# The first batch's columns by 16-bit halves and a transposing DMA, and three rows of the second batch's mixing by summands

## The chip, the cores and the metric

The kernel runs on one core of a Trainium2 chip (trn2). The engines that matter here are TensorE (PE: matmuls and transposes, its weight loads shown as PEld), VectorE (DVE), ScalarE (ACT), GpSimd (POOL) and SyncE (SP, which issues DMAs). Each engine works through its own instructions in the order of the program and waits for others by semaphores, each wait being a count that another engine's semaphore has to reach. The metric is the device time of one execution in microseconds (us).

## The reference

Three layers run one after the other on two batches of 768 tokens with 512 channels. Cut to what matters:

```python
# attention: q, k, v (2, 8, 768, 64); a key is kept if global (pos < 8) or local (0 <= rel < 96)
x = attention(q, k, v).transpose(0, 2, 1, 3).reshape(B, S, 512)

def _moe_ref(x, w_tok1, w_tok2, w_ch1, w_ch2):     # the second layer
    xt = x.transpose(0, 2, 1)
    h = np.maximum(xt @ w_tok1, 0.0) @ w_tok2      # mixes the 768 tokens, through 256
    u = x + h.transpose(0, 2, 1)
    h2 = np.maximum(u @ w_ch1, 0.0) @ w_ch2        # mixes the 512 channels, through 1536
    return u + h2

def _moe2_ref(x, w_theta, w_tok_r, w_tok_i, w_ch): # the third layer
    theta = x @ w_theta
    y = w_tok_r @ (x * cos(theta)) + w_tok_i @ (x * sin(theta))
    u = x + y
    return u + np.maximum(u @ w_ch, 0.0)
```

The change lies in the second layer, between `u` (after the token mixing) and `u @ w_ch1`. That product contracts over channels, so TensorE needs `u` with channels on the partitions, that is, the columns of `u`, while `u` itself has tokens on the partitions.

## The kernel before, in words

A float32 number is kept as two halves, a high one and a low one (the rest), and a product is three matmuls, high by high, high by low and low by high (`mm3`, L96). The rows of each batch stay in SBUF as `x[b]`, six blocks s of 128 tokens by 512 channels.

**Attention and token mixing.** The program tests the two counts in the inputs and takes the band branch or the dense branch of an If; these inputs take the band branch. Its work is a list of N units, and the work of the second layer that is ready is put between them as fills. For batch b, `token_part` makes `mm1` (`mm1_b_tb`, two halves tb of 256, contraction over the six blocks); at its end ScalarE makes the high half of `h1[b]` (L706) and VectorE the low one (L708). `token_row` then makes one block of rows `mm2_b_s`, six matmuls over two summands t, and VectorE adds it into `x[b]` (L768). For batch 0 all of this lies inside the branch. For batch 1, `mm1` is the end of the branch and `mm2` stands behind the If, in `token_mix2`.

**Columns.** For batch 0, `turn_row` lets TensorE transpose a block of rows, four transposes of 128 by 128 into one PSUM tile `ut_0_s` (L799), and ScalarE and VectorE split it into the high and low half of the columns, `ut[0]` (`evac_split`, L706 and L712; the memory is that of `xh0` and `xl0`, and the rows carry these names). Blocks 0 to 3 are fills, blocks 4 and 5 stand behind the last matmul of `mm1`. For batch 1 the columns come later, in `channel_mix`, in another way: `columns_out` lets POOL cut the 32-bit words into two planes of 16-bit halves (L779) and SP issue a transposing DMA (L783), `halves_join` lets POOL put the halves together again (L789), and `columns_split` makes the high half by a ScalarE cast (L792) and the low one by a VectorE subtraction (L793).

**Channel mixing.** `channel_mix` makes, for each of twelve steps k, `gp_b_k_0` (512 columns of `ut[b]`, blocks 0 to 3, 12 matmuls) and `gp_b_k_1` (256 columns, blocks 4 and 5), each evacuated by ScalarE and VectorE into `g` (L706, L708). Both use the PSUM tag `t`, which has two buffers; attention's transposes (L484) and `ut` use the same tag. Then come 18 matmuls of the second product, `h2`.

**What sets the order.** The program is written under a manual schedule: each engine takes its instructions as the code emits them. The weights are converted to halves by jobs: `job_scale` (ScalarE, L139 and L140), `job_join` (VectorE L145 and L148, then POOL L149), `job_high` (ScalarE L157), `job_low` (VectorE L160). Each `tick` emits the next phase of the running jobs and begins another. Behind the If, `token_mix2` ticks after rows 1, 3 and 5, and `channel_mix` after each evacuation. Behind the If the semaphore counts are the same whichever branch was taken.

The functions that the change touches, and what calls them:

Of the kernel before, what the change touches and what calls it, by code (L numbers as in the profile page):

```python
# [83 lines left out]
class Build:  # L84
# [326 lines left out]
    def attention_band(self, pairs_pool, first, h1):  # L411
# [6 lines left out]
        with tc.tile_pool(name="au", bufs=2) as up, tc.tile_pool(name="aa", bufs=2) as ap:  # L418
# [127 lines left out]
            def columns(s):  # L546
                return functools.partial(self.turn_row, "t", 0, s)

# [5 lines left out]
            for s in range(4):  # L554
                fill[N - 2 + s].append(columns(s))
# [47 lines left out]
            for s in range(4, NS):  # L603
                columns(s)()

    def attention_dense(self, pairs_pool, first, h1):
# [4 lines left out]
        with tc.tile_pool(name="du", bufs=2) as up, tc.tile_pool(name="dm", bufs=1) as mp:  # L611
# [86 lines left out]
            for s in range(NS):  # L698
                self.token_row("m", h1, 0, s)
                self.turn_row("t", 0, s)  # L700
# [52 lines left out]
    def token_row(self, tag, h1, b, s):  # L753

        ps = self.ps.tile([P, E], F32, name="mm2_%d_%d" % (b, s), tag=tag)
        cs = slice(s * P, (s + 1) * P)
        self.mm3(
# [12 lines left out]
    def turn_row(self, tag, b, s):  # L770
        h, s0 = divmod(s * P, E)
        hi, lo = (t[h][:, :, s0 : s0 + P] for t in self.ut[b])
        self.turn_rows(tag, self.x[b][:, s, :], r(hi), r(lo), "ut_%d_%d" % (b, s))
# [20 lines left out]

    def turn_rows(self, tag, src, hi, lo, name):

        pt = self.ps.tile([P, NE, P], F32, name=name, tag=tag)
        for d in range(NE):
            self.nc.tensor.transpose(pt[:, d, :], src[:, d * P : (d + 1) * P], self.ident)  # L799
        self.evac_split(hi, lo, pt)  # L800
# [66 lines left out]
    def run(self):  # L867
        nc, tc, dram = self.nc, self.tc, self.dram
        with ExitStack() as es:
# [13 lines left out]
            self.mm1 = {}  # L883
# [109 lines left out]
    def moe(self, es, a8s, w12p, h1):  # L993
        tc = self.tc
        ws = es.enter_context(tc.tile_pool(name="ws", bufs=1, side="right"))
        self.moe_jobs(ws, w12p)
        self.prefetch()
# [7 lines left out]
    def token_mix2(self, h1):  # L1005
        for s in range(NS):
            self.token_row("acc", h1, 1, s)
            if s % 2:
                self.tick()

    def columns_out(self, pb, s):
        t = self.turning[s] = pb.scratch("ut_%d" % s, ("cut", "xt0", "xt1")[s % 3])
        self.halves_out(self.x[1][:, s, :], t, self.nc.gpsimd.tensor_copy)

    def columns_split(self, s):
        h, s0 = divmod(s * P, E)
        hi, lo = (u[h][:, :, s0 : s0 + P] for u in self.ut[1])
        self.halves_split(self.turning.pop(s), r(hi), r(lo))
# [343 lines left out]
```

## Time and profile before

| | before |
|---|---|
| median of 3 runs | 497.35 us (497.07 to 498.65) |
| the profiled execution | 497.5 us, of which the span is 495.7 us |
| TensorE busy | 486.2 us, 98% of the span |
| VectorE, ScalarE, POOL busy | 312.6, 264.8, 180.8 us |
| mean granted TensorE clock | 0.996 |
| attention ends, second layer goes on behind the If | about 115 us |

The profile is one execution of the kernel. Its page sums the engines, follows the chain that ended last back through what released each piece, and groups the instructions by line. From the same trace come views of a stretch: the timeline (one row for one or more equal instructions in a row, with the idle time before the first and what ended it), the chain of a stretch, the instructions of one tile or one line, and tables of windows with the busy time of each engine and the granted clock of TensorE, where 1.00 is 2.4 GHz and 0.50 is 1.2 GHz. Spans on POOL are rough.

### The profile page before, as it was taken

Reading aid. Unit: us, or ns where it says so; the run is one execution under the profiler, and the core shown is the slowest. Engines: PE = TensorE matmul, PEld = TensorE weight load, DVE = VectorE, ACT = ScalarE, POOL = GpSimd, SP = SyncE. Lnnn points to the kernel's source line nnn. Section 1 sums busy time; section 2 is a strip of 40 time slices with the busy share of each in tenths; the row PEclk is TensorE's granted clock in tenths of the full one; section 3 lists DMA queues with packets and bytes.
Section 4 is the critical chain, followed back from the end, with each engine's and each line's share of the span. In section 5 each row is a group of like instructions: output and inputs, shape, how many; then the busy total and the mean of one; then the engine's idle time right before and its main releaser. Section 6 shows DMA issues by size and latency. Waiting matters only on the chain.

```text
span 495.7 us, 7653 instructions
## 1 busy us (share of the span) xinstructions
PE 486.2 (98%) x2836; PEld 413.8 (83%) x2836; DVE 312.6 (63%) x671; ACT 264.8 (53%) x482; POOL 180.8 (36%) x187
## 2 busy tenths in 40 slices
PE   8999999999999999999999999999997999999997
PEld 5788878787888888888888888888886889888896
DVE  4688878845767698416466564676877675651442
ACT  6788778723655555213577546647665655432010
POOL 7445443420343666301333151354444453333000
PEclk9999999999999999999999999999998999999999
DMA  7787764302454545202445131514410001100012
GB/s 201 207 254 244 246 217 125 105 2 82 134 171 101 157 123 154 64 1 71 117 131 181 53 105 44 150 42 107 106 22 22 22 22 22 42 22 22 22 66 104
DMA packets 49022, 50.66 MB, mean 102 GB/s; under 512 B 20944, under 2 KB 39888, under 8 KB 48976
## 3 DMA queue, kind: packets, MB, share of 16 engines
q1 hardware_dynamic: 48976, 50.08, 34.8%
q8 instruction: 25, 0.41, 0.4%
q14 instruction: 21, 0.17, 0.1%
HBM read 42.21 MB, written 3.15 MB: 91 GB/s over the span
## 4 chain that ended last, share of the span: by engine, by line
PE 84%; DVE 7%; ACT 4%; DMA 2%; POOL 1%; SPq 1%; issue 1%; DVEq 0%; ACTq 0%; POOLq 0%
PE gp L96 20%; PE h L96 18%; PE y L96 14%; PE v L96 7%; PE mm L96 7%; PE o L406 6%; PE th L96 5%; PE t L484 4%; PE s L437 4%; DMA k<-k 1%; DVE w L1170 1%; DMA q<-q 1%; DVE cvs L145 1%; DVE xt L793 1%; DVE x L1061 1%
## 5 line engine op out<-in xcount | busy, mean ns | idle before, releaser
L149 POOL TENSOR_TENSOR cvt<-cvt,cvs 128x512 int32<-128x512 int32 (+1 forms) x57 | 75.5, 1325 | 189.9 <-DVE cvt L148 168.2
L96 PE MATMUL h<-wc,g 128*128 128x512 f32 x432 | 101.7, 389 | 0.0
L96 PE MATMUL gp<-xh,wc 128*128 128x512 f32 (+1 forms) x384 | 97.1, 335 | 0.0
L96 PEld LDWEIGHTS h<-wc,g 128*128 128x128 f32 x432 | 79.6, 188 | 15.2
L96 PEld LDWEIGHTS gp<-xh,wc 128*128 128x128 f32 x384 | 67.3, 189 | 8.6 <-DVE g L708 0.2
L708 DVE SCALAR_TENSOR_TENSOR g<-gp,g 128x512 fp32r<-128x512 f32 (+1 forms) x48 | 26.7, 556 | 64.7 <-ACT g L706 64.5
L96 PE MATMUL gp<-xl,wc 128*128 128x512 f32 (+1 forms) x192 | 64.3, 335 | 0.0
L96 PE MATMUL y<-wri,s 128*128 128x256 f32 (+1 forms) x288 | 53.7, 344 | 2.7 <-ACT s L1171 1.5
L96 PEld LDWEIGHTS y<-wri,s 128*128 128x128 f32 x288 | 46.2, 196 | 9.2 <-ACT s L1171 1.9
L96 PE MATMUL y<-wri,z 128*128 128x256 f32 (+1 forms) x288 | 52.0, 335 | 0.0
L706 ACT ACTIVATE g<-gp 128x512 fp32r<-128x512 f32 (+1 forms) x48 | 23.4, 487 | 52.7 <-PE gp L96 52.7
L96 PEld LDWEIGHTS y<-wri,z 128*128 128x128 f32 x288 | 44.6, 188 | 6.1 <-POOL z L1173 0.2
L484 PE MATMUL t<-ident,e 128*128 128x128 f32 x176 | 48.1, 285 | 0.4 <-ACT at L496 0.4
L145 DVE SCALAR_TENSOR_TENSOR cvs<-cvt,cvs 128x512 int32<-128x512 int32 (+1 forms) x57 | 44.8, 787 | 0.0
L96 PEld LDWEIGHTS gp<-xl,wc 128*128 128x128 f32 x192 | 36.1, 188 | 4.6
L484 PEld LDWEIGHTS t<-ident,e 128*128 128x128 f32 x176 | 31.7, 184 | 8.1 <-issue 2.0
L450 DVE CUSTOM_DVE_ANT_0 e<-s,base 128x256 f32<-128x256 f32 (+1 forms) x96 | 32.9, 397 | 8.7 <-PE s L437 7.3
L139 ACT ACTIVATE cvt<-raw 128x512 f32<-128x512 f32 (+1 forms) x57 | 37.2, 652 | 2.2 <-issue 2.2
L140 ACT ACTIVATE cvs<-raw 128x512 int32<-128x512 uint16 (+1 forms) x57 | 37.2, 653 | 0.0
L96 PE MATMUL th<-s,xt 128*128 128x512 f32 x144 | 35.0, 392 | 0.0
L406 PE MATMUL o<-v,at 128*128 128x65 f32 x192 | 32.3, 252 | 0.0
L96 PEld LDWEIGHTS th<-s,xt 128*128 128x128 f32 x144 | 26.3, 189 | 5.2 <-DVE g L708 0.4
(111 smaller groups left out, 817.2 us busy)
## 6 DMA issues: line engine op xcount, KB each, us to landing
raw<-w_ch SPq DMA_DIRECT2D x28, 512.0 KB, 4.2
raw<-w_tok SPq DMA_DIRECT2D x21, 512.0 KB, 4.1
k<-k SPq DMA_DIRECT2D x7, 480.0 KB, 5.8
v<-v SPq DMA_DIRECT2D x8, 384.0 KB, 3.9
out<-o SPq DMA_DIRECT2D x11, 256.0 KB, 2.1
q<-q SPq DMA_DIRECT2D x7, 384.0 KB, 5.0
raw<-w_theta SPq DMA_DIRECT2D x4, 512.0 KB, 4.0
a<-v SPq DMA_DIRECT2D x8, 240.0 KB, 4.6
```

What stands on the lines that cost most here:

```text
L96: self.nc.tensor.matmul(out, lhsT=a, rhs=b, start=first and i == 0, stop=last and i == n - 1)
L139: nc.scalar.activation(out=f(t), in_=f(top), func=AF.Copy, scale=2.0**-111)
L140: nc.scalar.activation(out=s, in_=nxt, func=AF.Copy, scale=2.0**-13)
L145: nc.vector.scalar_tensor_tensor(out=s, in0=t, scalar=-(1 << 31), in1=s, op0=ALU.bitwise_and, op1=ALU.bitwise_or)
L149: nc.gpsimd.tensor_tensor(out=t, in0=t, in1=s, op=ALU.add)
L406: self.nc.tensor.matmul(po[:, j * OW : j * OW + D + 1], lhsT=at, rhs=v[:, j * (D + 1) : (j + 1) * (D + 1)], start=first, stop=last,)
L437: nc.tensor.matmul(ps[j][:, ii, c0:], lhsT=t["q"][pj, i * P : (i + 1) * P], rhs=kf[pj, i * KW - P + c0 : i * KW + P], start=True, stop=True,)
L450: nc.vector.tensor_tensor_reduce(out=e, in0=ps[j][:, ii, c0:], in1=self.base[2 * hp + j][min(i, 1)], op0=ALU.add, op1=ALU.min, scale=-SCAL ...
L484: nc.tensor.transpose(pt[:, ii, c, :], e[j][:, ii, c * P : (c + 1) * P], self.ident)
L706: nc.scalar.activation(out=hi, in_=ps, func=AF.Relu if relu else AF.Copy)
L708: nc.vector.scalar_tensor_tensor(out=lo, in0=ps, scalar=0.0, in1=f(hi), op0=ALU.max, op1=ALU.subtract)
L793: self.nc.vector.tensor_tensor(out=lo, in0=t[:, 1], in1=f(hi), op=ALU.subtract)
```

## The change

Batch 0's columns are made as batch 1's are. `turn_row` and `turn_rows`, and with them the 24 transposes of TensorE and the six PSUM tiles `ut_0_s`, are gone from both branches. Behind the If, `token_mix2` first emits for all six blocks the POOL copy and the transposing DMA (tiles `cut_u0_s`, in slots of the weight tag `w`), then the rows of batch 1's mixing, and between these rows the POOL join and the split of each block. Rows 0 to 2 of that mixing now go through the first summand in all three, then through the second; rows 3 to 5 go whole as before. The ticks stay after blocks 1, 3 and 5. `columns_out` and `columns_split` take the batch as an argument, and batch 1's own use of them is the same as before.

The diff, cut to its core:

```diff
-            def columns(s):
-                return functools.partial(self.turn_row, "t", 0, s)
...
-            for s in range(4):
-                fill[N - 2 + s].append(columns(s))
...
-            for s in range(4, NS):
-                columns(s)()
...
-    def token_row(self, tag, h1, b, s):
-
-        ps = self.ps.tile([P, E], F32, name="mm2_%d_%d" % (b, s), tag=tag)
+    def token_row(self, tag, h1, b, s, parts=range(NT)):
+
         cs = slice(s * P, (s + 1) * P)
+        if 0 in parts:
+            self.mm2[b, s] = self.ps.tile([P, E], F32, name="mm2_%d_%d" % (b, s), tag=tag)
+        ps = self.mm2[b, s]
...
-                for t in range(NT)
+                for t in parts
             ],
-        )
-        x = self.x[b][:, s, :]
-        self.nc.vector.tensor_tensor(out=x, in0=ps, in1=x, op=ALU.add)
...
+            first=0 in parts,
+            last=NT - 1 in parts,
+        )
+        if NT - 1 in parts:
+            x = self.x[b][:, s, :]
+            self.nc.vector.tensor_tensor(out=x, in0=ps, in1=x, op=ALU.add)
...
     def token_mix2(self, h1):
+        copy = self.nc.gpsimd.tensor_copy
         for s in range(NS):
-            self.token_row("acc", h1, 1, s)
+            t = self.ws.tile([P, 2, NE, P], F32, name="cut_u0_%d" % s, tag="w", bufs=9)
+            self.columns_out(0, s, t)
+        for t in range(NT):
+            for s in range(NS // 2):
+                self.token_row("acc", h1, 1, s, [t])
+        for s in range(NS):
+            if s >= NS // 2:
+                self.token_row("acc", h1, 1, s)
+            self.halves_join(self.turning[0, s], copy)
+            self.columns_split(0, s)
             if s % 2:
                 self.tick()
...
-    def columns_out(self, pb, s):
-        t = self.turning[s] = pb.scratch("ut_%d" % s, ("cut", "xt0", "xt1")[s % 3])
-        self.halves_out(self.x[1][:, s, :], t, self.nc.gpsimd.tensor_copy)
-
-    def columns_split(self, s):
+    def columns_out(self, b, s, t):
+        self.turning[b, s] = t
+        self.halves_out(self.x[b][:, s, :], t, self.nc.gpsimd.tensor_copy)
+
+    def columns_split(self, b, s):
```

POOL, behind the jump out of the If, before. `cvt` and `cvs` are the two parts of a weight that a conversion job joins at L149.

```order
L149 TENSOR_TENSOR cvt72_7517<-cvt72_7517,cvs73_7518 128x512
L149 TENSOR_TENSOR cvt75_7542<-cvt75_7542,cvs76_7543 128x512
L149 TENSOR_TENSOR cvt78_7569<-cvt78_7569,cvs79_7570 128x512
L149 TENSOR_TENSOR cvt81_7607<-cvt81_7607,cvs82_7608 128x512
L149 TENSOR_TENSOR cvt84_7634<-cvt84_7634,cvs85_7635 128x512
```

The same place after, where L771 is the copy into halves and L781 the join:

```order
L771 COPY cut_u0_3_7426<-x0_65 128x1024
L771 COPY cut_u0_4_7429<-x0_65 128x1024
L771 COPY cut_u0_5_7432<-x0_65 128x1024
L781 COPY cut_u0_0_7417<-cut_u0_0_7417 128x2x512
L781 COPY cut_u0_1_7420<-cut_u0_1_7420 128x2x512
L781 COPY cut_u0_2_7423<-cut_u0_2_7423 128x2x512
L781 COPY cut_u0_3_7426<-cut_u0_3_7426 128x2x512
L149 TENSOR_TENSOR cvt72_7465<-cvt72_7465,cvs73_7466 128x512
L781 COPY cut_u0_4_7429<-cut_u0_4_7429 128x2x512
L781 COPY cut_u0_5_7432<-cut_u0_5_7432 128x2x512
L149 TENSOR_TENSOR cvt75_7488<-cvt75_7488,cvs76_7489 128x512
```

Twelve POOL copies now stand ahead of the second job's L149, and the first job's L149 stands between the joins of blocks 3 and 4.

ScalarE at the same place, before (L139 and L140 begin a job, L157 makes a weight's high half, L706 evacuates `gp_0_0_0`):

```order
L139 ACTIVATE cvt72_7517<-raw70_7497 128x512
L140 ACTIVATE cvs73_7518<-raw70_7497 128x512
L139 ACTIVATE cvt75_7542<-raw71_7499 128x512
L140 ACTIVATE cvs76_7543<-raw71_7499 128x512
L157 ACTIVATE wc2_0_7564<-cvt72_7517 128x512
L139 ACTIVATE cvt78_7569<-raw74_7521 128x512
L140 ACTIVATE cvs79_7570<-raw74_7521 128x512
L706 ACTIVATE g_0_0_7585<-gp_0_0_0_7586 128x512
```

And after, where L784 is the cast and L698 the evacuation:

```order
L139 ACTIVATE cvt72_7465<-raw70_7413 128x512
L140 ACTIVATE cvs73_7466<-raw70_7413 128x512
L784 CAST xh0_70<-cut_u0_2_7423 128x4x128
L784 CAST xh0_70<-cut_u0_3_7426 128x4x128
L139 ACTIVATE cvt75_7488<-raw71_7415 128x512
L140 ACTIVATE cvs76_7489<-raw71_7415 128x512
L784 CAST xh0_70<-cut_u0_4_7429 128x4x128
L784 CAST xh0_70<-cut_u0_5_7432 128x4x128
L157 ACTIVATE wc2_0_7516<-cvt72_7465 128x512
L139 ACTIVATE cvt78_7521<-raw74_7469 128x512
L140 ACTIVATE cvs79_7522<-raw74_7469 128x512
L698 ACTIVATE g_0_0_7537<-gp_0_0_0_7538 128x512
```

The casts of all six blocks (those of 0 and 1 stand just ahead of the rows shown) come before the first evacuation, two of them between one job's beginning and the next.

VectorE after, behind the first three adds of `mm2_1` (L765; L785 is the subtraction that makes a block's low half, L700 an evacuation):

```order
L785 TENSOR_TENSOR xl0_71<-cut_u0_2_7423,xh0_70 128x4x128
L765 TENSOR_TENSOR x1_66<-mm2_1_3_7474,x1_66 128x512
L785 TENSOR_TENSOR xl0_71<-cut_u0_3_7426,xh0_70 128x4x128
L145 SCALAR_TENSOR_TENSOR cvs73_7466<-cvt72_7465,cvs73_7466 128x512
L148 TENSOR_SCALAR cvt72_7465<-cvt72_7465 128x512
L765 TENSOR_TENSOR x1_66<-mm2_1_4_7494,x1_66 128x512
L785 TENSOR_TENSOR xl0_71<-cut_u0_4_7429,xh0_70 128x4x128
L765 TENSOR_TENSOR x1_66<-mm2_1_5_7505,x1_66 128x512
L785 TENSOR_TENSOR xl0_71<-cut_u0_5_7432,xh0_70 128x4x128
L145 SCALAR_TENSOR_TENSOR cvs76_7489<-cvt75_7488,cvs76_7489 128x512
L148 TENSOR_SCALAR cvt75_7488<-cvt75_7488 128x512
L700 SCALAR_TENSOR_TENSOR g_0_0_7537<-gp_0_0_0_7538,g_0_0_7537 128x512
```

Before, the adds and the jobs stood here alone; now the first job's L145 and L148 follow the subtraction of block 3, and the evacuation of `gp_0_0_0` follows that of block 5.

## Rows read from the trace of the kernel before

**Rows 1.** The page: busy us (share) of each engine; the chain's shares by engine.

```profile
PE 486.2 (98%) x2836; PEld 413.8 (83%) x2836; DVE 312.6 (63%) x671; ACT 264.8 (53%) x482; POOL 180.8 (36%) x187
PE 84%; DVE 7%; ACT 4%; DMA 2%; POOL 1%; SPq 1%; issue 1%; DVEq 0%; ACTq 0%; POOLq 0%
```

**Rows 2.** The chain, 105 to 125 us: start us, us, what.

```profile
105.66 0.44 PE ut L799 x4
106.09 8.22 PE mm L96 x36
114.34 0.60 ACT h L706
114.94 0.50 ACT xh L706
115.43 0.41 issue
115.84 8.46 PE mm L96 x36
```

**Rows 3.** The timeline of PE: start us, us, instruction, [idle before, releaser].

```profile
97.88 0.33 PE L484 MATMUL t<-ident,e 128*128 128x128 f32 x1 [0.38 <-ACT at L496]
```

**Rows 4.** The timeline of all engines, 114 to 131 us.

```profile
114.97 0.69 DVE L708 SCALAR_TENSOR_TENSOR h<-mm,h 128x512 fp32r<-128x512 f32 x1 [0.67 <-ACT h L706]
...
118.16 0.66 ACT L139 ACTIVATE cvt<-raw 128x512 f32<-128x512 f32 x1 [2.24 <-issue]
...
119.10 1.91 DVE L768 TENSOR_TENSOR x<-mm,x 128x512 f32<-128x512 f32 x3 [2.25 <-PE mm L96]
...
122.22 0.68 DVE L145 SCALAR_TENSOR_TENSOR cvs<-cvt,cvs 128x512 int32<-128x512 int32 x1
122.94 0.43 DVE L148 TENSOR_SCALAR cvt<-cvt 128x512 int32<-128x512 int32 x1
...
123.51 1.29 POOL L149 TENSOR_TENSOR cvt<-cvt,cvs 128x512 int32<-128x512 int32 x1 [17.01 <-DVE cvt L148]
...
124.84 0.63 ACT L157 ACTIVATE wc<-cvt 128x512 fp32r<-128x512 f32 x1 [4.35 <-POOL cvt L149]
...
127.69 0.69 DVE L708 SCALAR_TENSOR_TENSOR g<-gp,g 128x512 fp32r<-128x512 f32 x1 [1.60 <-ACT g L706]
...
128.43 0.19 PEld L96 LDWEIGHTS gp<-xh,wc 128*128 128x128 f32 x1 [0.20 <-DVE g L708]
...
129.21 0.37 ACT L706 ACTIVATE g<-gp 128x256 fp32r<-128x256 f32 x1
...
130.13 0.42 DVE L708 SCALAR_TENSOR_TENSOR g<-gp,g 128x256 fp32r<-128x256 f32 x1
```

**Rows 5.** The If's own line, 104 to 120 us: duration ns min/median/max, start us.

```profile
L918 PEldq COMPARE_BRANCH  x1: 3887/3887/3887, 111.9 to 111.9; - x1
```

**Rows 6.** Batch 1's tile `cut_ut`: ns min/median/max, first and last start.

```profile
L779 POOL COPY cut_ut<-x x6: 1037/1262/1491, 155.3 to 199.4; 128x1024 uint16<-128x1024 uint16 x6
...
L789 POOL COPY cut_ut<-cut_ut x6: 1344/1598/1841, 163.5 to 203.8; 128x1024 uint16<-128x1024 uint16 x6
...
L793 DVE TENSOR_TENSOR xl<-cut_ut,xh x6: 678/936/1194, 171.3 to 207.7; 128x512 fp32r<-128x512 f32 x6
...
DMA to landing us min/median/max: 2.7/2.7/3.4
```

**Rows 7.** The timeline, where a join and a subtraction run side by side.

```profile
171.26 1.19 DVE L793 TENSOR_TENSOR xl<-cut_ut,xh 128x512 fp32r<-128x512 f32 x1 [0.79 <-ACT xh L792]
171.84 1.84 POOL L789 COPY cut_ut<-cut_ut 128x1024 uint16<-128x1024 uint16 x1
```

**Rows 8.** The page's DMA issues: KB each, median us from issue to landing.

```profile
raw<-w_ch SPq DMA_DIRECT2D x28, 512.0 KB, 4.2
```

**Rows 9.** Windows: us, busy us (instructions) of PE to POOL, granted clock, DMA share, GB/s.

```profile
373.50:375.20 1.70, 0.50 (x3) 0.29 (x3) 0.00 (x0) 1.67 (x2) 1.70 (x3) 1.00 0.00 0
...
376.00:379.40 3.40, 3.40 (x19) 3.40 (x18) 3.30 (x5) 1.05 (x1) 0.36 (x1) 0.50 0.07 15
```

More of the change, by code (lines that the diff above doesn't have):

```diff
@@ L699, in attention_dense @@
                 self.token_row("m", h1, 0, s)
-                self.turn_row("t", 0, s)
     def evac_split(self, hi, lo, ps, relu=False):
@@ L763, in token_row @@
                 )
-                for t in range(NT)
+                for t in parts
             ],
-        )
-        x = self.x[b][:, s, :]
-        self.nc.vector.tensor_tensor(out=x, in0=ps, in1=x, op=ALU.add)
[L770 to L773, printed above, removed]
+            first=0 in parts,
+            last=NT - 1 in parts,
+        )
+        if NT - 1 in parts:
+            x = self.x[b][:, s, :]
+            self.nc.vector.tensor_tensor(out=x, in0=ps, in1=x, op=ALU.add)
     def halves_out(self, src, t, copy):
@@ L793, in halves_split @@
         self.nc.vector.tensor_tensor(out=lo, in0=t[:, 1], in1=f(hi), op=ALU.subtract)
[L795 to L800, printed above, removed]
     def token_jobs(self):
@@ L882, in run @@
                 self.ut.append((self.columns_of(2 * b, hi), self.columns_of(2 * b + 1, lo)))
-            self.mm1 = {}
+            self.mm1, self.mm2 = {}, {}
             self.ps = Banks(es.enter_context(tc.tile_pool(name="ps", bufs=1, space=PSUM)))
@@ L996, in moe @@
         self.moe_jobs(ws, w12p)
+        self.turning = {}
         self.prefetch()
@@ L1005, in token_mix2 @@
     def token_mix2(self, h1):
+        copy = self.nc.gpsimd.tensor_copy
         for s in range(NS):
-            self.token_row("acc", h1, 1, s)
+            t = self.ws.tile([P, 2, NE, P], F32, name="cut_u0_%d" % s, tag="w", bufs=9)
[8 more added lines that the diff above has]
+            self.columns_split(0, s)
             if s % 2:
                 self.tick()
-    def columns_out(self, pb, s):
-        t = self.turning[s] = pb.scratch("ut_%d" % s, ("cut", "xt0", "xt1")[s % 3])
-        self.halves_out(self.x[1][:, s, :], t, self.nc.gpsimd.tensor_copy)
-    def columns_split(self, s):
+    def columns_out(self, b, s, t):
+        self.turning[b, s] = t
+        self.halves_out(self.x[b][:, s, :], t, self.nc.gpsimd.tensor_copy)
+    def columns_split(self, b, s):
         h, s0 = divmod(s * P, E)
-        hi, lo = (u[h][:, :, s0 : s0 + P] for u in self.ut[1])
-        self.halves_split(self.turning.pop(s), r(hi), r(lo))
+        hi, lo = (u[h][:, :, s0 : s0 + P] for u in self.ut[b])
+        self.halves_split(self.turning.pop((b, s)), r(hi), r(lo))
     def channel_mix(self, gp, pb):
@@ L1063, in channel_mix @@
         g = up(*steps[0])
-        self.turning = {}
         plan = {2: [(pb.turn_out, 0)], 3: [(pb.turn_in, 0), (pb.turn_out, 1)], 4: [(pb.turn_in, 1)],
@@ L1071, in channel_mix @@
                 if 0 <= k - 4 < NS:
-                    self.columns_split(k - 4)
+                    self.columns_split(1, k - 4)
                 if 0 <= k - 3 < NS:
-                    self.halves_join(self.turning[k - 3], nc.gpsimd.tensor_copy)
+                    self.halves_join(self.turning[1, k - 3], nc.gpsimd.tensor_copy)
                 if 0 <= k - 2 < NS:
-                    self.columns_out(pb, k - 2)
+                    s = k - 2
+                    self.columns_out(1, s, pb.scratch("ut_%d" % s, ("cut", "xt0", "xt1")[s % 3]))
             if b == 1:
```

## The prediction, made before the change was run

> **What bounds the kernel now.** I read the page's sums and its chain first: TensorE is busy for 98% of the span and carries 84% of the chain that ended last [rows 1]. So time is won only where TensorE waits or does avoidable work, and any stretch in which it is made to wait is lost for good, because nothing behind it has slack to give back. Then I read the chain of waits around the place of the change: behind `mm1_1` (the `mm` of batch 1's first product) stand the high half of its result on ScalarE, a copy of turned columns on ScalarE, 0.41 of issue, and then the 36 matmuls of `mm2_1` [rows 2]. Last came the timeline, for durations and for how each engine restarts behind the jump out of the If [rows 4], and the earlier uses of the same copy, transpose and join for batch 1 [rows 6, 7]. Times below are us on before's axis.
>
> **What goes.** 24 TensorE transposes, a row of four 0.44 [rows 2], 2.64 in all. Four rows stand as fills in attention, where the chain runs mostly through TensorE: 1.76. One wait of 0.38 there follows the turn of row 1 [rows 3]; `ut` takes a buffer of the tag that attention's own transposes use, so the wait may go too, or it may grow by the work that it covered. That bounds the gain in attention by 1.3 and 2.1; I take 1.85, the four rows and a quarter of the wait, since a ScalarE copy released it. The other eight transposes (0.88) and the gap stand behind `mm1_1`. TensorE's own jump began at 111.9 and took 3.89 [rows 5]; moved forward by 1.85 and by the missing 0.88 it ends near 113.1, so `mm2_1` starts about 113.1 instead of 115.84 and its 36 matmuls, at the 8.2 to 8.5 that 36 take [rows 2], end near 121.4. If nothing else mattered the gain were 2.7.
>
> **What comes.** Per 128-row block s, a POOL copy `cut` into 16-bit halves (1.04 at the least), an SP transpose (2.7 from issue to landing), a POOL join (1.34 at the least), a ScalarE cast (0.60, as any 128x512 there [rows 2]) and a VectorE subtraction (0.68 at the least) [rows 6]. The six transposes hide: the first four land before the sixth copy ends. The POOL copies and joins take 6 x 1.04 + 6 x 1.34 = 14.3, and they do not hide, for three reasons in the order of the instructions.
>
> First, copies 4 and 5. They stand behind the If, where their wait for row 4 or 5 of `x0` is one count of VectorE's semaphore that has to do for both branches. In the dense branch the last six VectorE operations are the adds into `x0`; in the band branch the same counts fall on attention's last operations. Copy 5 thereby waits for the subtraction that ends `h1_1`: 114.97 + 0.69 = 115.66 before [rows 4], 113.81 after. It ends at 114.9. POOL works in order, so all joins stand behind it. Had the copies gone at once, they would have ended near 113.1: POOL's restart behind the jump does not show before, as its next operation waited 17.01 [rows 4], but even 3 us for it from 104 lets six copies end there.
>
> Second, joins 0 to 3 in a row: 114.9 + 4 x 1.34 = 120.2. VectorE's subtractions of the same columns run beside them, and the trace shows what that costs: three of the six joins took 1.84, each beside such a subtraction of 1.19 (one pair is shown), where alone they take 1.34 and 0.68 [rows 6, 7]. I charge 0.5 once: 120.7. The Trainium skill, "SBUF — State Buffer", section "Who interferes with whom", says that a VectorE operation with two SBUF inputs and a GpSimd operation that reads SBUF exclude each other entirely; that speaks against this change and agrees with the 1.84 and 1.19. By it the sum stays as it is; without such a lock it would be the first rival below. Then the cast of block 3 ends at 121.3. VectorE has block 2 still to subtract (0.69), the add of `mm2_1_3` (0.69), and block 3 (0.69): 123.1. ScalarE and VectorE are there in time: behind the jump each sat idle 2.2 for "issue" or the like, and its first operation came at 118.16 and 119.10 [rows 4], moved forward with attention's end.
>
> TensorE could begin `gp_0_0_0` (blocks 0 to 3) at 121.4 and has its columns at 123.1, some 1.7 of waiting; it works until about 125.6, still earlier than before.
>
> Third, the conversion job stands on POOL between joins 3 and 4. Its addition at L149 waits for VectorE's L145 and L148 (0.68 and 0.43), which stand behind block 3's subtraction: 124.2. Then 1.29 for L149 [rows 4], join 4 and join 5 at 1.29 to 1.34: 128.1. Cast 5 ends at 128.8; VectorE does block 4 (1.19, beside join 5), the add of `mm2_1_5` and block 5: 130.0. `gp_0_0_1`, the second half, needs it. TensorE idles some 4, and finishes that half about 131.4.
>
> What is late next is the evacuation of `gp_0_0_0`. PSUM gives these products two buffers, so `gp_0_1_0` cannot start before it; before, TensorE's weight load stood at 128.43, released by exactly that VectorE operation [rows 4]. After, ScalarE does cast 5 (128.8), L157 (0.63), L139 (0.66) and L140 (as long as L139) before the high half (0.60): 130.9; VectorE's low half (0.69) ends at 131.7. So `gp_0_1_0` starts at 131.75: **3.3 late**. The evacuation of `gp_0_0_1` then stands behind the next job: its L145 and L148 follow block 5's subtraction (131.05), L149 ends at 132.4, L157, L139 and L140 at 134.3, the halves of 256 columns (0.37 and 0.42 [rows 4]) at 135.0, where TensorE wants the buffer 12 matmuls (a third of 8.2) after 131.75, at 134.5: **0.55 more**. From there TensorE is fed again, as before.
>
> The order by summand lets three matmuls of row 0 start before the second half of `h1_1` is whole. Row 1's first matmul carries a wait for that half's low part again by the same counts, so it covers 0.7 at most, and as TensorE waits for columns later, it is worth nothing. SP's six transposes stand ahead of the third weight load; that load then goes out near 116.2, and these loads' 4.2 to landing [rows 8] puts it at 120.4, before its use at 129.2: nothing.
>
> **The clock.** Later in the same run TensorE idled, worked 0.50 us in a stretch of 1.70, and then its granted clock was 0.50 (1.2 GHz) for 3.40 before it was 1.00 (2.4 GHz) again [rows 9]. The 4 us idle here may do the same. What it can slow is the 1.4 of `gp_0_0_1`: at half clock it ends 1.4 later, of which 0.35 falls into the wait for the buffer. Bounds 0 and 1.05; I take 0.3, near the lower end, as part of a slow stretch would fall on the idle time itself.
>
> **Sum.** The profiled execution took 497.5 (span 495.7 and 1.8 around it), the median of the runs shown is 497.35, 0.15 below. 497.5 + 3.3 + 0.55 + 0.3 - 0.15 = **501.5**.
>
> **Rivals.**
> *No lock.* If joins and subtractions run side by side at 1.34 and 0.68, block 5 ends about 1.3 earlier (joins 0 to 3 by 0.5, two subtractions by 0.5 each, partly in a row) and the evacuation behind it likewise; with L160 and L145 at 0.68 the second wait shrinks to 0.1. Loss 2.3, time 499.7. Against it: the pair in [rows 7].
> *Turned in time.* The other side: TensorE keeps its 2.7. It is decided at `gp_0_0_1`: block 5's subtraction has to end by 113.1 + 8.2 + 2.7 = 124.0. That takes copy 5 released by its data (near 113.1), six joins back to back (121.1) and block 5 right behind. Time 497.35 - 2.7 = 494.65; halfway 496. For it: POOL was idle 17.0 before its first work there [rows 4]. Against it: L149 stands between joins 3 and 4 and follows VectorE's order, which alone puts block 5 past 126.
> *A wash.* Copies released early and the evacuation not behind the tick: the loss falls to 0.9 or so, and a larger gain in attention (2.1) takes most: within 0.3%, which is 1.5 us, about what a measurement of this kernel can tell from no change.
> *Clock and locks at their worst.* 1.05 instead of 0.3, and 0.5 for each of three more joins: up to 503.8.
>
> **How the numbers follow.** Forecast 0.53, no lock 0.18, worst 0.12: these 0.83 are slower by over 0.3%. A wash 0.08. Turned in time 0.09. Range: from 498.8, below the no-lock case with the larger attention gain (499.4), to 503.9, above the worst; about 0.17 lies below it and a few hundredths above.
>
> **What would show it.** After: no `ut`; copies 4 and 5 of `cut_u0` just behind the last `h` subtraction, all joins later; L149 between joins 3 and 4; a TensorE wait of some 4 for `xl` in `gp_0_0_1`, then short ones for `g`; the last TensorE work of batch 0 about 3.9 later. It is wrong if copies 4 and 5 start before the subtraction of `h1_1`, if joins stay at 1.34 beside subtractions, or if TensorE's waits before 136 come to less than about 6.

## The result, and the profile after

The changed kernel takes 502.17 us in the median (501.44 to 503.11), the kernel before beside it 497.32; the ratio is 1.0093, with a 95% interval of 1.0067 to 1.0119. The profiled execution of the changed kernel took 502.57 and its span is 500.8, against 497.5 and 495.7. The forecast was 501.5 in a range of 498.8 to 503.9. One execution of the kernel with three blocks, told of below, took 678.85 at a mean granted clock of 0.657 against 0.993 to 1.000 in its other eleven; it is a slow execution and stands in no number here.

The page of the changed kernel, the lines that answer [rows 1]: busy us, share of the span and instructions of each engine; then the chain's shares by engine.

```profile
PE 487.2 (97%) x2812; PEld 412.9 (82%) x2812; DVE 313.0 (63%) x671; ACT 264.8 (53%) x482; POOL 194.3 (39%) x199
PE 83%; DVE 8%; ACT 3%; POOL 3%; issue 2%; DVEq 0%; POOLq 0%; ACTq 0%
```

TensorE lost 24 instructions and yet is busy for 1.0 longer: some of its work ran at a lower clock (a mean of 0.989 against 0.996). POOL is busy for 13.5 longer and stands on the chain with 3% instead of 1%.

Where the time went is read at one landmark, the first 18 matmuls of the second product `h2`. This is the chain of the kernel before there (start us, us, what):

```profile
124.30 8.56 PE gp L96 x48
132.86 4.08 PE h L96 x18
```

And this is the chain of the changed kernel, 112 to 142 us:

```profile
112.50 1.04 POOL cut_u L771
...
113.87 0.41 POOL cut_u L771
...
114.85 5.19 POOL cut_u L781 x4
120.03 3.99 issue
124.14 1.15 issue
125.30 1.34 POOL cut_u L781
126.66 0.63 ACT xh L784
127.31 1.04 DVE xl L785
...
128.95 0.61 DVE xl L785
129.60 8.09 PE gp L96 x35
137.69 4.08 PE h L96 x18
```

At the landmark the changed kernel is 4.83 late (137.69 against 132.86), and 5.1 at the end of the span. Before, this stretch of the chain was TensorE alone (the 48 matmuls of `gp` and then those of `h2`). Now it is POOL's copies of blocks 4 and 5, four joins, the job's L149 in the middle ("issue" of 3.99 and 1.15 ahead of and in it, in which POOL waits for VectorE and then adds), the last joins, then the cast and the subtractions. TensorE comes back at 129.60, and its 35 matmuls of `gp` take 8.09.

The timeline of the changed kernel, with the idle time before an instruction and what ended it:

```profile
105.16 3.99 POOL L771 COPY cut_u<-x 128x1024 uint16<-128x1024 uint16 x4 [0.15 <-DVE x L765]
...
112.41 0.96 PE L96 MATMUL mm<-h,w 128*128 128x512 f32 x3
...
113.11 0.69 DVE L700 SCALAR_TENSOR_TENSOR h<-mm,h 128x512 fp32r<-128x512 f32 x1 [0.67 <-ACT h L698]
...
113.86 7.78 PE L96 MATMUL mm<-h,w 128*128 128x512 f32 x33 [0.49 <-DVE h L700]
...
117.92 1.89 DVE L765 TENSOR_TENSOR x<-mm,x 128x512 f32<-128x512 f32 x3 [4.11 <-PE mm L96]
118.03 1.14 ACT L784 CAST xh<-cut_u 128x512 fp32r<-128x512 f32 x2 [4.95 <-POOL cut_u L781]
...
119.72 2.00 DVE L785 TENSOR_TENSOR xl<-cut_u,xh 128x512 fp32r<-128x512 f32 x3
...
122.97 0.50 PE L96 MATMUL gp<-xl,wc 128*128 128x512 f32 x1 [1.07 <-DVE xl L785]
...
124.06 1.29 POOL L149 TENSOR_TENSOR cvt<-cvt,cvs 128x512 int32<-128x512 int32 x1 [4.03 <-DVE cvt L148]
...
128.56 0.58 PE L96 MATMUL gp<-xh,wc 128*128 128x256 f32 x1 [2.79 <-ACT xh L784]
129.60 0.58 PE L96 MATMUL gp<-xl,wc 128*128 128x256 f32 x1 [0.47 <-DVE xl L785]
```

TensorE waits 0.49, 1.07, 2.79 and 0.47, together 4.82, where it had waited 0.66 and 0.2. VectorE works without a gap from its first add at 117.92 until past L148, so it is VectorE's late return, not POOL's joins, that holds L149 in this execution: join 3 ended at 120.04. The row of 113.11 answers that of 114.97 in [rows 4] and the row of 113.86 the 115.84 of [rows 2]; the rows of 117.92 and 118.03 answer those of 119.10 and 118.16 in [rows 4], and the row of 124.06 that of 123.51.

A window of the changed kernel (us, busy us of PE, PEld, DVE, ACT and POOL, the granted clock, DMA share, GB/s):

```profile
130.00:131.00 1.00, 1.00 (x6) 1.00 (x6) 0.90 (x3) 0.64 (x2) 0.31 (x1) 0.50 0.07 16
```

Late in the wait of 2.79 the clock falls to 0.50 (1.2 GHz), and further windows show it there from 128.0 to 134.5: TensorE works through `gp_0_0_1` and much of `gp_0_1_0` at half pace. In before there is no such stretch here; its only one is that of [rows 9].

### The profile page after: what moved, and what is told of

It is laid out like the page before. It is cut to its first block, busy times and chain, and to the rows that moved or that the text cites. A ratio compares the mean times of both kernels' runs of the same rounds, so it can differ in the third digit from the quotient of the medians.

```text
span 500.8 us, 7640 instructions
## 1 busy us (share of the span) xinstructions
PE 487.2 (97%) x2812; PEld 412.9 (82%) x2812; DVE 313.0 (63%) x671; ACT 264.8 (53%) x482; POOL 194.3 (39%) x199
## 4 chain that ended last, share of the span: by engine, by line
PE 83%; DVE 8%; ACT 3%; POOL 3%; issue 2%; DVEq 0%; POOLq 0%; ACTq 0%
PE gp L96 20%; PE h L96 18%; PE y L96 14%; PE v L96 7%; PE o L406 6%; PE s L437 5%; PE mm L96 5%; PE th L96 4%; PE t L484 4%; POOL cut_u L781 1%; DVE w L1166 1%; PE warm L330 1%; DVE cvs L145 1%; DVE xt L785 1%; DVE x L1057 1%
## 5 line engine op out<-in xcount | busy, mean ns | idle before, releaser
L149 POOL TENSOR_TENSOR cvt<-cvt,cvs 128x512 int32<-128x512 int32 (+1 forms) x57 | 75.3, 1321 | 178.2 <-DVE cvt L148 159.5
L96 PE MATMUL gp<-xh,wc 128*128 128x512 f32 (+1 forms) x384 | 99.2, 341 | 2.8 <-ACT xh L784 2.8
L96 PEld LDWEIGHTS gp<-xh,wc 128*128 128x128 f32 x384 | 68.8, 193 | 12.0 <-ACT xh L784 3.4
L700 DVE SCALAR_TENSOR_TENSOR g<-gp,g 128x512 fp32r<-128x512 f32 (+1 forms) x48 | 26.7, 556 | 64.9 <-ACT g L698 64.7
L96 PE MATMUL gp<-xl,wc 128*128 128x512 f32 (+1 forms) x192 | 65.6, 342 | 1.5 <-DVE xl L785 1.5
L698 ACT ACTIVATE g<-gp 128x512 fp32r<-128x512 f32 (+1 forms) x48 | 23.4, 487 | 53.6 <-PE gp L96 53.6
L145 DVE SCALAR_TENSOR_TENSOR cvs<-cvt,cvs 128x512 int32<-128x512 int32 (+1 forms) x57 | 44.8, 786 | 0.0
L140 ACT ACTIVATE cvs<-raw 128x512 int32<-128x512 uint16 (+1 forms) x57 | 37.4, 655 | 0.0
L139 ACT ACTIVATE cvt<-raw 128x512 f32<-128x512 f32 (+1 forms) x57 | 37.2, 653 | 0.0
```

Source lines behind the costliest of these rows:

```text
L96: self.nc.tensor.matmul(out, lhsT=a, rhs=b, start=first and i == 0, stop=last and i == n - 1)
L139: nc.scalar.activation(out=f(t), in_=f(top), func=AF.Copy, scale=2.0**-111)
L140: nc.scalar.activation(out=s, in_=nxt, func=AF.Copy, scale=2.0**-13)
L145: nc.vector.scalar_tensor_tensor(out=s, in0=t, scalar=-(1 << 31), in1=s, op0=ALU.bitwise_and, op1=ALU.bitwise_or)
L149: nc.gpsimd.tensor_tensor(out=t, in0=t, in1=s, op=ALU.add)
L698: nc.scalar.activation(out=hi, in_=ps, func=AF.Relu if relu else AF.Copy)
```

## The experiments

The theory is that of the prediction; the rivals are told with each run. Medians and ratios to the kernel before, which ran beside each:

| kernel | median us | ratio to before (95%) |
|---|---|---|
| the changed kernel | 502.17 | 1.0093 (1.0067 to 1.0119) |
| rows 0 to 2 whole | 502.94 | 1.0108 (1.0083 to 1.0133) |
| other order of the dense branch | 502.12 | 1.0083 (1.0058 to 1.0109) |
| no transposing DMAs | 501.47 | 1.0078 (1.0053 to 1.0103) |
| two ticks | 499.34 | 1.0041 (1.0024 to 1.0058) |
| dense order and two ticks | 501.12 | 1.0080 (1.0059 to 1.0100) |
| 12 matmuls in the wait | 501.72 | 1.0101 (1.0081 to 1.0121) |
| 10 matmuls in the wait | 501.27 | 1.0083 (1.0068 to 1.0098) |
| before, with the order by summand | 497.12 | 0.9996 (0.9987 to 1.0006) |
| two blocks by DMA | 496.45 | 0.9991 (0.9981 to 1.0001) |
| three blocks by DMA | 498.16 | 1.0017 (1.0002 to 1.0032) |
| four blocks by DMA | 500.22 | 1.0061 (1.0046 to 1.0075) |
| all six inside attention | 504.61 | 1.0161 (1.0140 to 1.0182) |

**The order by summand: undone, and alone.** First undone in the changed kernel:

```diff
-        for t in range(NT):
-            for s in range(NS // 2):
-                self.token_row("acc", h1, 1, s, [t])
         for s in range(NS):
-            if s >= NS // 2:
-                self.token_row("acc", h1, 1, s)
+            self.token_row("acc", h1, 1, s)
             self.halves_join(self.turning[0, s], copy)
```

> The changed kernel with rows 0 to 2 of mm2_1 whole again instead of by summands. Theory (the columns of batch 0 are late: POOL's copies and joins, the job's L149 between them, the evacuation of gp_0_0_0 behind them): TensorE starts mm2_1 about 0.5 to 0.7 later, and waits that much less for the columns, so the time stays within 0.4 of the changed kernel's 502.2. Rival (the order of the matmuls is what moved the time): at least 0.7 away from it, to 497.3 if the order were the whole of it.

The median is 502.94, 0.8 above the changed kernel's and so outside the 0.4, but not towards before as the rival would have it; the two ranges overlap (501.95 to 503.62, 501.44 to 503.11), and its profiled execution, the fastest of its four, is at the landmark 0.6 earlier than the changed kernel's, at 137.07. So the two can't be told apart. Then the order alone, in the kernel before (`token_row` and `token_mix2` as in the change, without the copies, joins and splits):

> The kernel before with the order by summand alone; the columns are turned by TensorE as before. Theory: mm2_1's first matmul was released there by the last copy of turned columns and by TensorE's own jump (115.78), not by the second half of h1_1, so the order moves nothing: within 0.4 of before's 497.3. Rival (the order lets TensorE start earlier): 0.5 to 0.7 faster.

497.12 beside 497.17: nothing. Three matmuls do go ahead of the wait in the changed kernel (the row of 112.41), as the diff says, but TensorE then waits for columns that are no earlier for it. The order is not where the time went.

**Copies 4 and 5 released.** In the branch that doesn't run, batch 0's rows go ahead of batch 1's first product:

```diff
                 for tb in range(NT):
                     for s in range(NS):
                         self.token_part("m", h1, bb, tb, s)
-            for s in range(NS):
-                self.token_row("m", h1, 0, s)
+                if bb == 0:
+                    for s in range(NS):
+                        self.token_row("m", h1, 0, s)
```

> The changed kernel; in the dense branch, which doesn't run, batch 0's rows are mixed ahead of batch 1's first product, so that the counts that copies 4 and 5 wait for fall on the adds into x0 in the band branch as well. Theory: copy 5 ends near 111.4 instead of 114.9, join 0 starts there and not at 114.85, join 5 ends about 1.7 to 2.5 earlier than 127.9; gp_0_0_1 starts at 126 to 127 instead of 128.56; 499.5 to 500.8. Rival (POOL's start is hidden behind VectorE's and ScalarE's late restart): joins early, but the subtractions still from 119.7 on, and the time within 0.5 of 502.2.

The timeline of this kernel:

```profile
107.66 5.95 POOL L772 COPY cut_u<-x 128x1024 uint16<-128x1024 uint16 x6 [2.81 <-PE mm L96]
...
117.38 2.71 POOL L782 COPY cut_u<-cut_u 128x1024 uint16<-128x1024 uint16 x2 [0.33 <-DMA cut_u<-cut_u]
...
117.83 1.89 DVE L766 TENSOR_TENSOR x<-mm,x 128x512 f32<-128x512 f32 x3 [4.18 <-PE mm L96]
...
124.13 1.29 POOL L149 TENSOR_TENSOR cvt<-cvt,cvs 128x512 int32<-128x512 int32 x1 [4.04 <-DVE cvt L148]
```

The six copies now run in one piece and end at 113.6, not at 114.9: in the changed kernel copies 4 and 5 were indeed held (its chain's pieces of 112.50 and 113.87). But POOL's first copy came 2.5 later than there, and the joins then waited for landings, so that join 3 ended at 120.09, no earlier than the 120.04 of the changed kernel. VectorE's first add behind the jump is where it was (117.83 against 117.92), and so is L149. The median is 502.12, within the rival's 0.5 of 502.2, and my 499.5 to 500.8 was wrong. But the rival's condition, early joins, was met by the first join alone. What four joins ended early would give was not tested; the timeline of the changed kernel, where VectorE is busy from 117.92 on, speaks for the rival.

The row of 107.66 names TensorE as what ended the 2.81 of idle time before the first copy. With both fixes, below, the same 2.81 stands there, and in the kernels with the same order of the dense branch and two, three and four blocks turned by TensorE it is 1.67, 0.64 and 0.20. A wait that shrinks with TensorE's work in the branch looks like a count of TensorE's semaphore that the new order moved, as the old one held copies 4 and 5; this is argued, not tested.

**Why VectorE and ScalarE restart late.** Before, VectorE's first add came 3.1 after its branch, the last record of the jump; in the changed kernel it came 4.8 after. The six transposing DMAs are left out, and the copy writes into the plane that the join reads:

```diff
         copy(
-            out=a.rearrange("p (w n) -> p w n", w=2),
+            out=(a if dma else b).rearrange("p (w n) -> p w n", w=2),
...
-        self.nc.sync.dma_start_transpose(out=b.rearrange("p (m x) -> p m x", x=P), in_=a)
+        if dma:
+            self.nc.sync.dma_start_transpose(out=b.rearrange("p (m x) -> p m x", x=P), in_=a)
```

> The changed kernel without the six transposing DMAs of batch 0 (the copy writes straight into the plane that the join reads, so batch 0's columns hold wrong values). It asks why ScalarE and VectorE did nothing until 118.0 and 117.9 behind the jump, 5.5 and 4.8 after their branch, where it was 2.9 and 3.1 before. Theory (the six transposes keep the DMA engines busy from 108 to 118, and the fetch of the instructions behind the jump stands behind them): first operations at about 115.4 to 116.2 on both, TensorE's jump 3.9 instead of 4.13; the time falls by 0.3 to 1.2, since the joins from 114.9 on still set the end. Rival (they wait for copies, joins or TensorE's rows): no first operation before 117.5, time within 0.3 of 502.2.

The timeline of this kernel:

```profile
115.88 0.62 ACT L785 CAST xh<-cut_u 128x512 fp32r<-128x512 f32 x1 [3.15 <-POOL cut_u L782]
115.96 2.04 DVE L765 TENSOR_TENSOR x<-mm,x 128x512 f32<-128x512 f32 x3 [2.51 <-PE mm L96]
```

Both are 2.0 to 2.2 earlier than in the changed kernel; VectorE is back 3.2 after its branch at 112.8, close to before. The rows name a join and a matmul as what ended the waits, so the restart itself took no longer than that. L149 came only 0.53 earlier, at 123.53: VectorE now subtracted beside the joins, and three subtractions took 3.27 instead of 2.00. The queues' rows of a DMA view of 112 to 119 us show the fetched instructions themselves (packets, MB, share of 16 engines in that stretch). The changed kernel:

```profile
q1 hardware_dynamic: 3720, 0.93, 113.6%
q14 instruction: 3, 0.02, 4.3%
```

The kernel without transposes:

```profile
q14 instruction: 4, 0.03, 1.6%
```

A share of 4.3% of sixteen engines in 7 us is 4.8 us for three packets, 1.6 each; without transposes it is 1.8 us for four, 0.45 each. So in the changed kernel the fetched instructions took three to four times as long among the small packets of the transposes. The Trainium skill, "Runtime: NRT & Kernel Launch", section "Instruction fetch mechanics", says that a taken branch whose target has not been prefetched forces a fetch by DMA before execution can go on. The traces agree in so far as such packets move in all three kernels there; the page gives no duration to hold against the 3.1.

That six transposes go with a later restart is what the runs add: VectorE came 2.9 to 3.2 after its branch in three kernels without transposes there, and 3.4 to 5.5 in seven with six. That the slower packets are the reason is not shown. With ten matmuls in the wait, below, VectorE came 5.0 after its branch, though four packets took 1.5% of the same stretch, as little as without transposes. The whole effect is a small part of the loss at most: 501.47 against 502.17, with ranges that overlap.

**L149 out of the joins' way.** One tick of the three between the rows is left out:

```diff
             self.columns_split(0, s)
-            if s % 2:
+            if s in (1, NS - 1):
                 self.tick()
```

> The changed kernel with two ticks of the weight jobs instead of three between the rows: one behind block 1, one behind block 5. So L149 leaves its place between joins 3 and 4, and L157 and a second pair of L139 and L140 leave their place ahead of the evacuation of gp_0_0_0; all later phases of the jobs come one tick later. Theory: joins 4 and 5 end near 122.6 instead of 127.9, gp_0_0_1 starts at 126 to 127 rather than 128.56, gp_0_1_0 at 128 to 129 instead of 132.3, the granted clock stays near 1.00 or falls for less than 2 us; 498 to 499.5. Rival (the jobs are needed so soon that a tick later costs as much): TensorE waits for wc at gp_0_2_0 instead, time above 501.

Its timeline, and then its chain at the landmark:

```profile
114.97 8.95 POOL L781 COPY cut_u<-cut_u 128x1024 uint16<-128x1024 uint16 x6
...
116.65 1.89 DVE L765 TENSOR_TENSOR x<-mm,x 128x512 f32<-128x512 f32 x3 [2.72 <-PE mm L96]
...
118.45 4.30 DVE L785 TENSOR_TENSOR xl<-cut_u,xh 128x512 fp32r<-128x512 f32 x3
...
124.48 0.50 PE L96 MATMUL gp<-xl,wc 128*128 128x512 f32 x1 [2.49 <-DVE xl L785]
```

```profile
133.50 4.12 PE h L96 x18
```

The landmark is at 133.50, 4.2 earlier than in the changed kernel and 0.64 later than before; `gp_0_0_1` no longer waits, and the clock stays at 1.00 there. The profiled execution is the fastest of the eight (498.44 to 501.15). The median falls by 2.8 to 499.34, near the upper end of what was expected. Of the median's loss of 4.85 leaving out the tick thus gave back more than half: L149 between the joins, the tick's work ahead of the evacuation, and the clock that follows from the wait, which this run does not separate. Nor does it separate VectorE's return, which came 1.27 earlier here (116.65 against 117.92) for a reason that isn't known. What is left is VectorE: three subtractions beside the joins take 4.30, where in the changed kernel, after its joins, the same three took 2.00, 0.77 less each. That is the pair of [rows 7] again, and TensorE waits 2.49 for it.

Both fixes together did not add up:

> All six blocks by DMA behind the jump as in the changed kernel, with both the other order of the dense branch (copies 4 and 5 not held) and two ticks instead of three. Theory (the parts of the loss stand in a row, so that releasing the copies shows nothing alone, but does once L149 is out of the joins' way): the subtraction of block 3 ends near 122.4 instead of 124.4 with two ticks alone, 497.3 to 498.4. Rival (held copies cost nothing in any company): 499.0 to 499.7, as with two ticks alone.

```profile
118.30 1.89 DVE L766 TENSOR_TENSOR x<-mm,x 128x512 f32<-128x512 f32 x3 [4.80 <-issue]
...
120.10 4.24 DVE L786 TENSOR_TENSOR xl<-cut_u,xh 128x512 fp32r<-128x512 f32 x3
...
125.60 0.80 PE L96 MATMUL gp<-xl,wc 128*128 128x512 f32 x1 [3.90 <-DVE xl L786]
```

501.12, outside both expectations. VectorE came back 1.65 later than with two ticks alone (118.30 against 116.65), the joins waited for landings and then stood beside the subtractions as before, TensorE waited 3.90, and the clock fell to 0.50 late in that wait. In this company leaving out the tick gave back 1.0 only (501.12 against the 502.12 of the other order of the dense branch), so what it is worth hangs on VectorE's return and on the clock. The return differs between kernels whose code is the same up to there: 4.8 after the branch in the changed kernel, 3.4 with two ticks, 4.1 and 5.0 with twelve and ten matmuls in the wait, below. Whether the 5.5 here is more than such chance is not settled.

**What the clock costs.** Matmuls on data at hand fill TensorE's wait:

```diff
+                if (b, k, h) == (0, 0, 0):
+                    self.keep_busy(12)
                 self.evac_split(g[:, 0, hs], g[:, 1, hs], ps, relu=True)
```

> The changed kernel with twelve matmuls added between gp_0_0_0 and gp_0_0_1, on data at hand, into a PSUM tile that nobody reads; they fill TensorE's wait for the columns of blocks 4 and 5 (2.8 before 128.56). Theory (after that wait the granted clock falls to 0.50, and this costs more than the 0.3 that was foreseen): the clock stays 1.00 from 128 to 135, gp_0_1_0 starts near 131.4 instead of 132.3, the first matmuls of h2 come at 136.2 to 136.6 instead of 137.7, and the time falls by 1.0 to 1.6, to 500.6 to 501.2. Rival (the clock falls for another reason, or the slow stretch hides in the wait for the buffer): time within 0.4 of 502.2.

> The changed kernel with ten matmuls instead of twelve in TensorE's wait ahead of gp_0_0_1, and more rounds, since the twelve moved the last matmul by 1.53 and the median by 0.45 only. Theory (the slow clock costs 1.0 to 1.5): clock 1.00 from 128 to 135, first matmuls of h2 at 136.0 to 136.5, the changed kernel's median of 502.17 less 1.0 to 1.5 is 500.7 to 501.2. Rival (what the clock gives back is lost elsewhere behind it): 501.5 to 502.2, with the last matmul of the profile nevertheless 1.3 to 1.6 earlier than in the changed kernel.

A window and the chain's rows of the kernel with ten:

```profile
129.00:132.00 3.00, 2.15 (x14) 1.86 (x15) 2.89 (x5) 1.65 (x5) 1.28 (x1) 1.00 0.33 51
```

```profile
136.17 4.09 PE h L96 x18
```

In both the clock stays at 1.00 there and the landmark comes 1.5 earlier (136.13 and 136.17 against 137.69). Now the two waits for evacuated buffers show that the slow clock had hidden: 0.27 ahead of `gp_0_1_0`, and `gp_0_1_1` after VectorE's evacuation that ends at 134.48. With ten the span is 1.7 shorter and the median 0.9 lower, 501.27; with twelve 0.7 and 0.45. Both medians lie between the two expectations. So the slow stretch costs 1.5 at its place in the profiled execution, and in the medians 0.5 to 0.9, which the intervals of the ratios don't tell from nothing (1.0083 and 1.0101 beside 1.0093). Of that difference a part is that the changed kernel's own executions differ in their mean granted clock (0.992 at 501.44 and 501.78, 0.989 at 502.57 and 503.11): the profiled one was of the slower pair. With twelve, 0.8 more goes after the last matmul, in the last output's landing; that is not settled.

**How many blocks have room.** Blocks 0 to 3 are turned by TensorE in attention again, blocks 4 and 5 go by DMA, with the joins ahead of L149:

```diff
+            for s in range(4):
+                fill[N - 2 + s].append(columns(s))
...
-        for s in range(NS):
+        for s in range(4, NS):
             t = self.ws.tile([P, 2, NE, P], F32, name="cut_u0_%d" % s, tag="w", bufs=9)
             self.columns_out(0, s, t)
...
-            self.halves_join(self.turning[0, s], copy)
-            self.columns_split(0, s)
+            if 2 <= s < 4:
+                self.halves_join(self.turning[0, s + 2], copy)
+                self.columns_split(0, s + 2)
```

> Half of the change: blocks 0 to 3 are turned by TensorE in attention as before; only blocks 4 and 5, whose transposes stood behind mm1_1, go by halves and transposing DMA, their joins ahead of the first job's L149. The order by summand and the other order of the dense branch are in it. Theory (the loss comes from six joins and casts in a row behind the jump, not from the way itself): mm2_1 starts near 115.0 instead of 115.84, blocks 4 and 5 are there by 122 to 123, ahead of gp_0_0_1 which is due near 126, no wait for columns, 496.2 to 496.9. Rival (the restart behind the jump and the jobs behind the joins cost as much whatever the number of blocks): TensorE waits for xl or g all the same, 498 or more.

```profile
117.89 5.44 PE mm L96 x24
123.33 8.56 PE gp L96 x48
131.89 4.08 PE h L96 x18
```

VectorE's first add of this kernel:

```profile
118.00 2.05 DVE L773 TENSOR_TENSOR x<-mm,x 128x512 f32<-128x512 f32 x3 [2.51 <-PE mm L96]
```

The chain of this kernel is TensorE alone again and 0.97 earlier than before at the landmark. The median is 496.45 against 497.17; the interval of the ratio, 0.9981 to 1.0001, just includes no change. Three and four blocks, with `range(4)` and the joins changed accordingly and all joins behind row 2:

> As the kernel with two blocks by DMA, but blocks 3, 4 and 5 go that way and blocks 0 to 2 are turned by TensorE in attention; the joins stand together ahead of the first job's L149. Theory (a block is free as long as its join, cast and subtraction end before TensorE asks for it; behind the jump there is room for three): mm1_1 starts 0.3 to 0.4 earlier, block 3 is there by 122, ahead of gp_0_0_0, and no wait follows; 495.9 to 496.3, a little below the 496.45 of two blocks. Rival (the restart behind the jump leaves room for two only): TensorE waits for xl at gp_0_0_0, 496.5 or more.

> Blocks 2 to 5 by DMA, blocks 0 and 1 by TensorE in attention. Theory: another 0.3 to 0.4 saved in attention, but four subtractions behind the first three adds end near 122.6 to 123.5, where TensorE asks for gp_0_0_0 near 122.2; a wait of 0.3 to 1.3; 495.9 to 496.9. Rival (room for all four): 495.5 to 495.9. If the loss grew with each block alike, 497.5 or more.

Two rows of the timeline with three blocks, and one with four:

```profile
118.97 1.89 DVE L773 TENSOR_TENSOR x<-mm,x 128x512 f32<-128x512 f32 x3 [3.45 <-PE mm L96]
...
128.75 0.50 PE L96 MATMUL gp<-xh,wc 128*128 128x512 f32 x1 [1.26 <-DVE g L708]
```

```profile
129.12 0.50 PE L96 MATMUL gp<-xh,wc 128*128 128x512 f32 x1 [1.92 <-DVE g L708]
```

498.16 and 500.22. The theory's times are missed, and the rivals' "496.5 or more" and "497.5 or more" are met for another reason than was written. TensorE doesn't wait for columns in either. It waits for the evacuation of `gp_0_0_0`, 1.26 and 1.92: the subtractions stand ahead of the first job's L145 on VectorE, so L149 starts at 124.41 and 124.78 instead of 123.08 with two blocks, and the evacuation stands behind L157 on ScalarE. I had looked at the columns only. But with three blocks 0.97 of that 1.33 is VectorE's return, 118.97 against 118.00, and 0.33 of the 1.70 with four is (118.33), which leaves less than half a microsecond of L149's delay to the third block itself. With four the clock then falls as well (0.61 in 129 to 132).

**All six inside attention.** Copies, joins and splits go into the units of the band branch, in the slots of the raw weight loads:

```diff
+                if 0 < s:
+                    fill[N - 4 + s].append(functools.partial(join, s - 1))
+                if 1 < s:
+                    fill[N - 4 + s].append(functools.partial(self.columns_split, 0, s - 2))
                 fill[N - 4 + s].append(mix2(s))
+                fill[N - 4 + s].append(functools.partial(out, s))
```

> All six blocks by halves and transposing DMA, but inside the band branch: each copy behind its row's add, each join one unit later, each cast and subtraction two units later, in the slots of the raw weight loads, which are free there. Nothing of it stands behind the jump. Theory: TensorE saves the transposes (1.4 in attention, 0.9 and the gap behind mm1_1) and never waits for columns; mm2_1 starts near 113.2 to 113.9, gp_0_0_0 near 121.5, 494.6 to 495.6. Rival (POOL's copies and joins hold VectorE's operations in attention, or casts that wait for joins hold ScalarE's exponentials): mm1_1 starts later than 103.6 and the time is 496.5 or more; above 498 if each of four units loses 1.

The chain of this kernel:

```profile
112.56 1.34 POOL cut L797
113.90 0.96 POOL cut L787
...
114.88 3.61 DMA cut<-cut
...
118.63 1.30 POOL cut L797
...
119.95 0.63 ACT xh L800
...
121.95 9.60 PE mm L96 x33
```

504.61: worse than the change, and on the rival's side. POOL becomes attention's pace: a join waits for its landing, the next copy waits behind the join, and the operations that make batch 1's halves wait behind both. The last of it is a landing of 3.61 in front of TensorE. The jump was not needed for the loss.

## Why the prediction was right, step by step

The sign and the time were right, 502.17 where 501.5 was said, and so was the mechanism in the main: the columns come late, L149 stands between the joins, and the evacuations come late behind them. But that the total is only 0.7 off is partly luck, as it hides errors that offset each other, and one of the prediction's own signs of being wrong came up. TensorE's waits before 136 were to come to no less than about 6; they come to 4.82. The wait for `gp_0_0_1` was 2.79 and 0.47, not 4, and the waits for `g` did not show, as the slow clock filled them.

- **Gain in attention.** 1.85 was taken; the subtraction that ends `h1_1` starts at 113.11 instead of 114.97 [rows 4], 1.86 earlier. The wait of 0.38 in [rows 3] is gone, one of 0.47 for VectorE's L399 is there instead.
- **Held copies.** The times were right: copy 5 was to end at 114.9 and join 0 to start there; it did at 114.85. As a cause it is not shown: releasing them gave nothing, but there the first copy came later and the joins ended no earlier.
- **Joins 0 to 3 and the lock.** 0.5 was charged and did not come: the four joins took 5.19, because VectorE's first add came at 117.92, 0.7 later than the 119.10 of [rows 4] moved forward by 1.85, and it began to subtract only at their end. Where the two do meet, as with two ticks, a subtraction takes 0.77 more. Of the later pair, join 5 and block 4's subtraction, only the subtraction grew, to 1.04; the two joins took 2.56 together. "Joins stay at 1.34 beside subtractions", another sign of being wrong, thus held for this one pair, though the price fell on the subtraction. Block 3's subtraction was said to end at 123.1 and TensorE's second matmul, which needs it, came at 122.97.
- **L149 between the joins.** Said to start at 124.2, measured 124.06; join 5 to end at 128.1, measured 127.9; `gp_0_0_1`'s low half said at 130.0, measured 129.60.
- **The evacuations.** Said to end at 131.7 and 135.0; without the slow clock they free the buffers at 131.41 and 134.5, which gives 136.17 at the landmark, 3.3 late, where 3.85 was the sum.
- **The clock.** This is the term that was mis-sized. 0.3 was taken, out of bounds of 0 and 1.05, "as part of a slow stretch would fall on the idle time itself". It did not: the slow stretch fell on `gp_0_0_1` and on `gp_0_1_0`, and cost 1.5. The bound of 1.05 was too low, because only the first of the two products was put in it.
- **Order by summand.** Said to be worth nothing; it is.

The 4.83 at the landmark thus splits into 3.3, with the clock held up by spare matmuls, and 1.5 that the slow clock adds, where the prediction had 3.85 and 0.3: 0.55 too much and 1.2 too little. The no-lock rival's condition held in the four joins, but its price, a loss of 2.3, didn't follow, because the row of waits goes through VectorE's late return and L149. The rival on the other side did not come up; the wash neither. With two blocks, where the waits are gone, the median is 0.7 lower than before, at the edge of what the interval tells from no change.

## What to carry to other kernels

Moving work from the busiest engine to idle ones pays only if every step of the new chain, and all that is queued behind it on each engine, ends before the busy engine asks: here two blocks of six went through without a wait; with three the median was 1.7 higher, and the wait was not for the columns but for the evacuation that stood behind them. Look for what stands between the steps in program order (here a job's L149 and a tick) before counting their durations; leaving out one tick gave back more than half of the loss, though in another company only a fifth. And price a wait of the matmul engine with the work that comes behind it at the lower clock, not with the wait alone.

## What the runs showed of the hardware

- VectorE's first operation came 2.9 to 3.2 us after its jump out of the If in three kernels without transposing DMAs there, and 3.4 to 5.5 in seven with six of them in flight. Fetched instruction packets took about 1.6 us each among them in the changed kernel and 0.45 without them; that this is the reason is not shown.
- Six transposing DMAs in a row landed after 4.6 in the median, where the single ones of [rows 6] took 2.7. This is the row of the changed kernel's tile:

```profile
DMA to landing us min/median/max: 2.8/4.6/5.8
```

- A subtraction with both inputs in SBUF took 0.67 alone and 1.43 on average in a row of three beside POOL's joins (4.30 against 2.00 for the three); the six joins took 8.95 there, where six at the 1.34 of [rows 6] are 8.04.
- During a wait of 2.79 on TensorE the granted clock fell to 0.50 and stayed there until 134.5, and matmuls on spare data in that wait kept it at 1.00.
